# Turning all of batch 1's attention output inside block 0, so that block 1's first product starts in 512 columns

## The chip, the cores and the metric

The kernel runs on one core of a Trainium2 chip. The metric is device time in microseconds of one execution. A profiled execution also gives a span, from its first instruction to its last, and the trace that the profile is read from. Engines are named as the profile names them: PE (matrix products and transposes), PEld (its weight loads), DVE and ACT (the two vector-like engines), POOL and SP (here mostly issuers of transfers).

## What is computed

Two stages follow each other. q, k and v have 8 batches, 8 heads, 576 positions and 64 features.

```python
q_p = concat(relu(q) * cos, relu(q) * sin)           # per position, 64 -> 128 features; k_p alike
kv  = einsum('bhsf,bhsd->bhfd', k_p, v)              # k^T v, one 128 x 64 matrix per head
z   = k_p.sum(axis=positions)
x   = (q_p @ kv) / (q_p @ z + 1e-6)                  # attention output, 576 x 512 per batch
h   = x @ w_in                                       # 512 -> 2048
out = (h * sigmoid(1.702 * h)) @ w_out               # 2048 -> 512
```

All inputs and the output are float32; the kernel computes its products in bf16 with float32 sums.

## The kernel before

The work is cut by batch into eight blocks. Of each batch's 576 positions 512 go through the block in four chunks of 128 (c = 0 to 3); the last 64 (c = 4) are put aside in `xt` and treated together for all batches at the end. The order of every engine's instructions is written out by hand (`manual_schedule`, line 48): an engine runs its instructions in the order of the program, and what it has to wait for is found from the tiles that it reads and writes.

The steps, by function:

- `trig` and `trig_q` make the relu times cos and sin features of k and q, in `kr` and `qn`; `vcopy(i0, i1)` (L157) casts v into `vt`, for head pairs i0 to i1, on DVE or with `act=True` on ACT.
- `qturn_pe(c)` (L167) turns chunk c of q with PE transposes into a PSUM tile, `qevac(c)` (L174) copies it into `qT` (on DVE, or on ACT with `act=True`). For batch 1 the PSUM tiles are the two halves of an `at` tile (`at_homes`, L183).
- `kv_mm` (L202, instructions at L207) is k^T v: 72 products of 64 rows by 65 columns. `kv_evac` (L210, L212) copies the result to `kvs` on DVE.
- `num_mm(c)` (L226, L230) multiplies chunk c of q by `kvs`, 8 products of 65 columns into an `at` tile. `num_div(c)` (L248) divides on DVE in three instructions: `den` (L236), `inv` (L238), `xn` (L254).
- `xturn_mm(c)` (L269, L274) turns `xn` with 4 PE transposes into a free part of the same `at` tile, and `xturn_evac(b, c)` (L276, L280) copies it to `xT` on ACT. `xturn_dma` (L282, L285) does the turning by a transfer from SP instead.
- `mm1(b, fc)` (L303) is one 128-wide slice of x times w_in: 4 products of 512 columns (`mm1_part`, L291, L295), and `gelu` (L300) on ACT into a `g` tile. A block has 16 slices. `mm1_part(b, fc, t0, t1)` can do the same for one chunk, 4 products of 128 columns.
- `mm2(b, t, lo, hi)` (L327, L332) adds slices lo to hi of the second product for chunk t, one 512-column product each. With hi = 16 the sum is complete: ACT copies it to `ysb` (L336) and POOL sends it out (L340).

PSUM has two pools: `pmm` with four buffers (products) and `pat` with two `at` buffers, handed out in turn. The third `at` tile asked for has to wait until the first has been read.

Block 0 is different from the others because batch 1's attention is worked in between its products. The 64 products of `mm2(0, ...)` (L458 to L503) are interleaved with batch 1's q transposes, k^T v, `num_mm` and the first transposes of x. When block 0's products end, two of the four chunks of batch 1's x are turned. `start_block(1, opened=True)` (L355) then begins block 1 chunk by chunk, in 128 columns, for its first four slices, and turns chunks 2 and 3 between these parts; `start_block(0)` does the same for block 0. Blocks 2 to 7 have their x turned by transfers during the block before, and run all 16 slices in 512 columns (L507 on).

Of the kernel before, what the change touches and what calls it, by code (L numbers as in the profile page):

```python
# [19 lines left out]
def kernel(  # L20
# [14 lines left out]
    FC = d_ff // 128  # L35
# [75 lines left out]
    def w_in_of(kc, fc):  # L111
        return w_in_v[fc // 4][:, kc, fc % 4, :]

    def load(t, src, b, eng=nc.gpsimd):
        eng.dma_start(out=t, in_=src_of(src, b))
# [41 lines left out]
    def vcopy(i0, i1, act=False):  # L157
        o = vt[:, :, i0:i1, 0:64].rearrange("p j i e -> p i j e")
        i = vf[:, i0:i1].rearrange("p i (j e) -> p i j e", e=64)
        if act:  # L160
            nc.scalar.activation(o, i, AF.Copy)
        else:
            nc.vector.tensor_copy(o, i)
# [10 lines left out]
    def qevac(c, act=False):  # L174
        n = min(2 * c + 2, NS) - 2 * c
        o = qT[:, :, ds(c * 128, n * 64)].rearrange("f h (j p) -> f j h p", j=n)
        i = tps.pop(c)[:, 0:n].rearrange("f j i (hh p) -> f j (i hh) p", hh=2)
        if act:
            nc.scalar.activation(o, i, AF.Copy)
        else:  # L180
            nc.vector.tensor_copy(o, i)

    def at_homes():  # L183
        t = pat.tile([128, 2, 512], F32, name="at")
        return [t[:, u].bitcast(BF16).rearrange("p (j i f) -> p j i f", j=2, i=NI) for u in range(2)]
# [24 lines left out]
    def kv_evac(i0, i1, n=65):  # L210
        o = st["kvs"][:, :, i0:i1, 0:n]
        nc.vector.tensor_copy(o, st["ps", i0].rearrange("p hh (i e) -> p hh i e", e=65)[:, :, :, 0:n])  # L212
# [13 lines left out]
    def num_mm(c):  # L226
        ps = pat.tile([128, 2, 512], F32, name="at")
        for h in range(H):
            i, hh = divmod(h, 2)
            nc.tensor.matmul(ps[:, h // 4, ds((h % 4) * 65, 65)], qT[:, h, ts(c, 128)],  # L230
                             st["kvs"][:, hh, i, 0:65], start=True, stop=True)
        nums[c] = [ps]
# [15 lines left out]
    def num_div(c, inv=None):  # L248
        ps = nums[c][0]
        pv = ps[:, :, 0:260].rearrange("p a (h e) -> p a h e", h=4)  # L250
        if inv is None:
            inv = inv_of(pv[:, :, :, 64])
        xn = small.tile([128, 2, 4, 64], BF16, name="xn", bufs=4)
        nc.vector.tensor_tensor(xn, pv[:, :, :, 0:64],  # L254
                                inv.unsqueeze(3).to_broadcast([128, 2, 4, 64]), op=MUL)
        nums[c].append(xn)
# [12 lines left out]
    def xturn_mm(c):  # L269
        ps, xn = nums[c]  # L270
        xv = xn.rearrange("p a h e -> p (a h e)")
        for kc in range(KC):
            o = ps[:, kc // 2, ds(264 + (kc % 2) * 64, 64)].bitcast(BF16)
            nc.tensor.transpose(o, xv[:, ts(kc, 128)], ident)  # L274

    def xturn_evac(b, c):  # L276
        ps = nums.pop(c)[0]
        i = ps[:, :, 264:392].bitcast(BF16).rearrange("p a (k t) -> p a k t", k=2)
        o = x_of(b, c).rearrange("p (a k) t -> p a k t", a=2)
        nc.scalar.activation(o, i, AF.Copy)  # L280

    def xturn_dma(b, c):  # L282
        xn = nums.pop(c)[1]
        n = 128 if c < 4 else 64
        nc.sync.dma_start_transpose(out=x_of(b, c), in_=xn[0:n].rearrange("p a h e -> p (a h e)"))  # L285
# [5 lines left out]
    def mm1_part(b, fc, t0, t1):  # L291
        if t0 == 0:
            hp[fc] = pmm.tile([128, MT], F32, name="mm")
        for kc in range(KC):
            nc.tensor.matmul(hp[fc][:, t0:t1], w_in_of(kc, fc), x[b][:, kc, t0:t1],  # L295
                             start=(kc == 0), stop=(kc == KC - 1))

    def gelu(fc):
        g = gpool.tile([128, MT], BF16, name="g")
        nc.scalar.activation(g, hp.pop(fc), AF.Gelu_apprx_sigmoid)  # L300
        gT[fc] = g

    def mm1(b, fc):  # L303
        mm1_part(b, fc, 0, MT)
        gelu(fc)
# [21 lines left out]
    def mm2(b, t, lo, hi, c0=0, c1=d_model):  # L327
        if lo == 0:
            yp[t, c0] = pmm.tile([128, d_model], F32, name="mm")
        for fc in range(lo, hi):  # L330
            w = gT[fc][:, ts(t, 128)] if t < 4 else gl_t[:, fc, ts(t - 4, 128)]
            nc.tensor.matmul(yp[t, c0][:, c0:c1], w, w_out_sb[:, fc, c0:c1],  # L332
                             start=(fc == 0), stop=(fc == FC - 1))
        if hi == FC:
            ysb = ypool.tile([128, d_model], F32, name="ysb")
            nc.scalar.activation(ysb[:, c0:c1], yp[t, c0][:, c0:c1], AF.Identity)  # L336
            for p0, n, dst in rows(b, t):
                last = b == B - 1 and t != 4 and (t, p0) != (5, 0)
                eng = nc.sync if last else nc.gpsimd
                eng.dma_start(out=dst[:, c0:c1], in_=ysb[p0:p0 + n, c0:c1])  # L340
# [11 lines left out]
    def vt_rhs(r, i, j):  # L352
        return vt[r, j, i, 0:65]

    def start_block(b, opened=False):  # L355

        if not opened:
            xturn_mm(0)
            xturn_evac(b, 0)
            num_mm(2)  # L360
            num_div(2)
            xturn_mm(1)
            xturn_evac(b, 1)
        def part(c, *fcs):
            for fc in fcs:
                mm1_part(b, fc, c * 128, c * 128 + 128)

        part(0, 0, 1, 2, 3)
        num_mm(3)
        num_div(3)  # L370
        xturn_mm(2)
        xturn_evac(b, 2)
        part(1, 0, 1, 2, 3)
        xturn_mm(3)
        xturn_evac(b, 3)
        num_mm(4)
        num_div(4)
        xturn_dma(b, 4)
        part(2, 0, 1, 2)
        part(3, 0, 1)  # L380
        part(2, 3)
        part(3, 2, 3)
        for fc in range(4):
            gelu(fc)
        mm1(b, 4)


    w = idle(12)
    for j in (0, 1):
        trig(kr, kf, j)  # L390
# [46 lines left out]
    qevac(4)  # L437
    idle(1)
    x_open(0)
    start_block(0)  # L440


    load(kf, k, 1)
# [15 lines left out]
        mm2(0, t, 0, 4)  # L459
    mm2(0, 0, 4, 8)  # L460
    mm2(0, 1, 4, 8)
    ha = at_homes()
    qturn_pe(0, ha[0])
    qturn_pe(1, ha[1])
    qevac(0)
    qevac(1, act=True)
    mm2(0, 2, 4, 8)
    mm2(0, 3, 4, 8)
    hb = at_homes()
    qturn_pe(2, hb[0])  # L470
    qturn_pe(3, hb[1])
    vcopy(0, 2)
    vcopy(2, 4, act=True)
    qevac(2)
    qevac(3, act=True)
    load_q(2, nc.gpsimd)
    load(kf, k, 2, nc.gpsimd)
    load(vf, v, 2, nc.gpsimd)
    mm2(0, 0, 8, 12)
    mm2(0, 1, 8, 12)  # L480
    hc = at_homes()
    qturn_pe(4, hc[0])
    qevac(4)
    kv_open()
    kv_mm(0, 4, vt_rhs, 0, 65)
    kv_evac(0, 4)
    mm2(0, 2, 8, 12)
    mm2(0, 3, 8, 12)
    num_mm(0)
    num_div(0)  # L490
    num_mm(1)
    num_div(1)
    x_open(1)
    mm2(0, 0, 12, 16)
    mm2(0, 1, 12, 16)
    xturn_mm(0)
    xturn_evac(1, 0)
    mm2(0, 2, 12, 16)
    xturn_mm(1)
    xturn_evac(1, 1)  # L500
    num_mm(2)
    num_div(2)
    mm2(0, 3, 12, 16)  # L503
    start_block(1, opened=True)


    for b in range(1, B):  # L507
        nb = b + 1 if b + 1 < B else None
        f0 = 5 if b == 1 else 0
        for fc in range(f0, FC):  # L510
            if nb is not None and fc == f0:
                for c in range(5):
                    trig_q(c)
                    qturn_dma(c)
                if nb + 1 < B:
                    load_q(nb + 1)
            if nb is not None and fc == f0 + 1:
                for j in range(NS if b > 1 else 5):
                    trig(kr, kf, j)
                vcopy(0, 4 if b > 1 else 2)  # L520
            mm1(b, fc)
            if b == 1 and fc in (7, 9, 11, 13):
                trig(kr, kf, (fc + 3) // 2, act=True)
        if b == 1:
            vcopy(2, 4, act=True)
        if nb is None:
            for fc in range(FC):
                mm1_tails(fc)
            for t in (4, 5, 6, 7):
                mm2(b, t, 0, FC)  # L530
            for t in range(3):
                mm2(b, t, 0, FC)
            mm2(b, 3, 0, FC, 0, 256)
            mm2(b, 3, 0, FC, 256, 512)
            continue
        x_open(nb)
        lag = 1 if b == 1 else 0
        for u in range(8):
            if u == lag:
                kv_open()  # L540
                kv_mm(0, 4, vt_rhs, 0, 65)
                kv_evac(0, 4)
            if 0 <= u - lag - 1 < 5:
                num_mm(u - lag - 1)
                num_div(u - lag - 1)
                xturn_dma(nb, u - lag - 1)
            mm2(b, u // 2, 8 * (u % 2), 8 * (u % 2) + 8)
        if nb + 1 < B:
            load(kf, k, nb + 1, nc.sync)
            load(vf, v, nb + 1, nc.sync)  # L550
# [30 lines left out]
```

## Time and profile before

| | us |
|---|---|
| median of 3 runs (lowest to highest) | 292.51 (292.34 to 292.56) |
| the profiled execution, its time | 292.51 |
| the profiled execution, its span | 290.8 |
| PE busy | 284.3 |
| ACT busy | 132.9 |
| DVE busy | 124.1 |
| POOL busy | 37.8 |

The span is 1.7 us shorter than the time of the same execution; what lies around the span is taken as constant. The profiled execution's time is also the median of the runs. In the timeline a row gives the start, the length from the first start to the last end, the engine, the line, the operation, the tiles as output<-input, and the number of instructions that the row merges. Products on PE overlap: one lasts longer than the distance to the next, so the cost of a group is read from its start to the start of the group after it.

### The profile page before, as it was taken

To read this page: it belongs to the slowest core of one execution; us is meant where nothing else is said; L and a number is where in the kernel's file an instruction comes from. 1 tells how busy PE (TensorE), PEld (TensorE's weight loads), DVE (VectorE), ACT (ScalarE), POOL (GpSimd) and SP (SyncE) were. 2 spreads that over 40 slices of the span, in tenths; PEclk is the share of its full clock that TensorE was granted. 3 is DMA by queue.
4 is the path that set the end of the run, shared out by engine and by line. 5 is a ranking of instruction groups with operands and counts; after the bars stand their busy time and mean duration, and the time that the engine had idled before them with its cause. 6 is when DMAs were issued, how large, how long until landed. Compare 5 with 4: busy or idle time off the path is not lost.

```text
span 290.8 us, 5789 instructions
## 1 busy us (share of the span) xinstructions
PE 284.3 (98%) x2330; PEld 154.8 (53%) x2330; DVE 124.1 (43%) x356; ACT 132.9 (46%) x232; POOL 37.8 (13%) x71
## 2 busy tenths in 40 slices
PE   7989999999999999999999999999999999999995
PEld 2775466755555554555455545554555455544444
DVE  4953645842648363826582567156624200000000
ACT  7957654693156214721463136412651167751111
POOL 6650044101210001001100110011000100002000
PEclk9999999999999999999999999999999999999999
DMA  7999999684689958975699469756975400002322
GB/s 250 244 214 287 372 267 363 172 181 128 126 225 306 220 132 276 260 197 145 225 277 227 122 192 335 184 143 152 379 94 74 117 36 3 0 0 44 87 88 72
DMA packets 67771, 52.48 MB, mean 180 GB/s; under 512 B 47969, under 2 KB 57953, under 8 KB 67745
## 3 DMA queue, kind: packets, MB, share of 16 engines
q1 hardware_dynamic: 60320, 32.52, 45.2%
q0 software_dynamic: 7424, 19.60, 23.6%
q8 instruction: 18, 0.29, 0.4%
q14 instruction: 9, 0.07, 0.1%
HBM read 36.70 MB, written 9.44 MB: 159 GB/s over the span
## 4 chain that ended last, share of the span: by engine, by line
PE 92%; DMA 5%; DVE 1%; POOL 1%; issue 0%; ACT 0%; ACTq 0%
PE mm L332 43%; PE mm L295 38%; PE mm L312 5%; DMA w_in<-in_moe_w_in_dram 3%; PE at L230 3%; PE at L207 3%; DMA kf<-in_k_dram 1%; PE at L171 1%; POOL vb L132 1%; DVE xn L254 0%; PE at L274 0%; DVE inv L238 0%; ACT ysb L336 0%; DVE den L236 0%; POOL gate L130 0%
## 5 line engine op out<-in xcount | busy, mean ns | idle before, releaser
L332 PE MATMUL mm<-w_out_sb,g 128*128 128x512 bf16 (+1 forms) x528 | 117.9, 373 | 0.0
L295 PE MATMUL mm<-xT,w_in 128*128 128x512 bf16 (+1 forms) x608 | 112.9, 345 | 0.2 <-DMA w_in<-in_moe_w_in_dram 0.2
L300 ACT ACTIVATE g<-mm 128x512 bf16<-128x512 f32 x128 | 75.1, 598 | 30.4 <-PE mm L295 30.2
L295 PEld LDWEIGHTS <-w_in 128*128 128x128 bf16 x608 | 61.6, 113 | 49.6 <-DMA w_in<-in_moe_w_in_dram 0.3
L332 PEld LDWEIGHTS <-g 128*128 128x128 bf16 x528 | 48.7, 97 | 49.6
L336 ACT ACTIVATE ysb<-mm 128x512 f32<-128x512 f32 (+1 forms) x37 | 21.7, 586 | 109.7 <-PE mm L332 106.7
L340 POOL DMA_DIRECT2D out_dram<-ysb x39 | 21.2, 547 | 205.6 <-ACT ysb L336 203.6
L142 DVE TENSOR_SCALAR kr<-kf,cosw 128x256 bf16<-128x256 f32 x64 | 22.5, 351 | 30.3 <-DMA kf<-in_k_dram 30.3
L254 DVE TENSOR_TENSOR xn<-at,inv 128x512 bf16<-128x512 f32 x40 | 27.7, 691 | 1.7 <-PE at L230 0.4
L142 DVE TENSOR_SCALAR kr<-kf,sinw 128x256 bf16<-128x256 f32 x64 | 22.6, 354 | 0.0
L236 DVE TENSOR_SCALAR den<-at 128x8 f32<-128x8 f32 x39 | 6.5, 166 | 34.4 <-PE at L230 34.4
L230 PEld LDWEIGHTS <-qT 128*128 128x128 bf16 x320 | 14.6, 97 | 8.1 <-issue 0.8
L212 DVE CAST kvs<-at 128x520 bf16<-128x520 f32 (+1 forms) x9 | 5.7, 635 | 28.9 <-PE at L207 28.9
L230 PE MATMUL at<-kvs,qT 128*128 128x65 bf16 x320 | 15.9, 193 | 0.7 <-ACT xT L280 0.7
L155 DVE TENSOR_SCALAR qn<-qf,sinw 128x512 bf16<-128x512 f32 (+1 forms) x30 | 14.4, 480 | 0.0
L155 DVE TENSOR_SCALAR qn<-qf,cosw 128x512 bf16<-128x512 f32 (+1 forms) x30 | 14.3, 476 | 0.0
L312 PE MATMUL mm<-xt,w_in 128*128 128x512 bf16 x64 | 14.0, 379 | 0.0
L332 PE MATMUL mm<-w_out_sb,gl_t 128*128 128x512 bf16 x64 | 14.0, 379 | 0.0
L313 ACT ACTIVATE gl_t<-mm 128x512 bf16<-128x512 f32 x16 | 9.6, 597 | 4.2 <-PE mm L312 4.2
L312 PEld LDWEIGHTS <-w_in 128*128 128x128 bf16 x64 | 7.2, 113 | 6.6
L207 PEld LDWEIGHTS <-kr 64*128 64x128 bf16 x576 | 9.3, 94 | 2.7 <-issue 2.5
L332 PEld LDWEIGHTS <-gl_t 128*128 128x128 bf16 x64 | 6.3, 98 | 7.5
(63 smaller groups left out, 115.4 us busy)
## 6 DMA issues: line engine op xcount, KB each, us to landing
kf<-in_k_dram SPq DMA_DIRECT2D x5, 1152.0 KB, 6.9
vf<-in_v_dram SPq DMA_DIRECT2D x5, 1152.0 KB, 9.6
qf<-in_q_dram SPq DMA_DIRECT2D x5, 1024.0 KB, 6.2
out_dram<-ysb POOLq DMA_DIRECT2D x20, 256.0 KB, 2.8
out_dram<-ysb POOLq DMA_DIRECT2D x19, 128.0 KB, 4.1
kf<-in_k_dram POOLq DMA_DIRECT2D x2, 1152.0 KB, 11.7
vf<-in_v_dram POOLq DMA_DIRECT2D x2, 1152.0 KB, 16.5
w_in<-in_moe_w_in_dram POOLq DMA_DIRECT2D x4, 512.0 KB, 10.2
```

The lines of the kernel that those rows point to most:

```text
L142: eng.tensor_scalar(o, i, 0.0, w[:, j:j + 1], op0=MAX, op1=MUL)
L155: nc.vector.tensor_scalar(o, i, 0.0, sc, op0=MAX, op1=MUL)
L207: nc.tensor.matmul(st["kv", i][:, hh, ds(col, n)], kr[r, j, i, :], rhs(r, i, j), start=(j == 0), stop=(j == NS - 1))
L230: nc.tensor.matmul(ps[:, h // 4, ds((h % 4) * 65, 65)], qT[:, h, ts(c, 128)], st["kvs"][:, hh, i, 0:65], start=True, stop=True)
L254: nc.vector.tensor_tensor(xn, pv[:, :, :, 0:64], inv.unsqueeze(3).to_broadcast([128, 2, 4, 64]), op=MUL)
L295: nc.tensor.matmul(hp[fc][:, t0:t1], w_in_of(kc, fc), x[b][:, kc, t0:t1], start=(kc == 0), stop=(kc == KC - 1))
L300: nc.scalar.activation(g, hp.pop(fc), AF.Gelu_apprx_sigmoid)
L312: nc.tensor.matmul(hps, w_in_of(kc, fc), xt[:, kc, :], start=(kc == 0), stop=(kc == KC - 1))
L313: nc.scalar.activation(gl_t[:, fc, :], hps, AF.Gelu_apprx_sigmoid)
L332: nc.tensor.matmul(yp[t, c0][:, c0:c1], w, w_out_sb[:, fc, c0:c1], start=(fc == 0), stop=(fc == FC - 1))
L336: nc.scalar.activation(ysb[:, c0:c1], yp[t, c0][:, c0:c1], AF.Identity)
L340: eng.dma_start(out=dst[:, c0:c1], in_=ysb[p0:p0 + n, c0:c1])
```

## The change

`start_block` is gone. Block 0's copy of it stands in line, with `num_mm(4)`/`num_div(4)` ahead of `xturn_mm(3)`/`xturn_evac(0, 3)`. In block 0's second product batch 1's k^T v moves up, directly behind q's turns 0 to 3, and both halves of `vcopy` of batch 1 go to DVE; q's turn 4 goes behind k^T v. `num_mm` of chunks 0 and 1 moves up into the third quarter (slices 8 to 12), and in the last quarter (slices 12 to 16) the `num_mm` of chunks 2, 3 and 4 and the x turns of chunks 1, 2 and 3 stand between the four groups of four products, so that all four chunks of batch 1's x are turned inside block 0. Block 1 then runs all its 16 slices in 512 columns.

```diff
-    def start_block(b, opened=False):
...
-        part(0, 0, 1, 2, 3)
-        num_mm(3)
-        num_div(3)
-        xturn_mm(2)
-        xturn_evac(b, 2)
-        part(1, 0, 1, 2, 3)
-        xturn_mm(3)
-        xturn_evac(b, 3)
-        num_mm(4)
-        num_div(4)
-        xturn_dma(b, 4)
-        part(2, 0, 1, 2)
...
-        mm1(b, 4)
...
-    start_block(0)
+    xturn_mm(0)
...
+    part(0, 0, 1, 2, 3)
+    num_mm(3)
+    num_div(3)
+    xturn_mm(2)
+    xturn_evac(0, 2)
+    part(1, 0, 1, 2, 3)
+    num_mm(4)
+    num_div(4)
+    xturn_mm(3)
+    xturn_evac(0, 3)
+    xturn_dma(0, 4)
+    part(2, 0, 1, 2)
...
+    mm1(0, 4)
...
     mm2(0, 0, 4, 8)
     mm2(0, 1, 4, 8)
+    mm2(0, 2, 4, 8)
     ha = at_homes()
     qturn_pe(0, ha[0])
     qturn_pe(1, ha[1])
     qevac(0)
     qevac(1, act=True)
-    mm2(0, 2, 4, 8)
+    vcopy(0, 2)
+    vcopy(2, 4)
     mm2(0, 3, 4, 8)
     hb = at_homes()
     qturn_pe(2, hb[0])
     qturn_pe(3, hb[1])
-    vcopy(0, 2)
-    vcopy(2, 4, act=True)
-    qevac(2)
+    qevac(2, act=True)
     qevac(3, act=True)
     load_q(2, nc.gpsimd)
     load(kf, k, 2, nc.gpsimd)
     load(vf, v, 2, nc.gpsimd)
+    kv_open()
+    kv_mm(0, 4, vt_rhs, 0, 65)
+    kv_evac(0, 4)
     mm2(0, 0, 8, 12)
-    mm2(0, 1, 8, 12)
     hc = at_homes()
     qturn_pe(4, hc[0])
     qevac(4)
-    kv_open()
-    kv_mm(0, 4, vt_rhs, 0, 65)
-    kv_evac(0, 4)
+    num_mm(0)
+    num_div(0)
+    mm2(0, 1, 8, 12)
+    num_mm(1)
+    num_div(1)
     mm2(0, 2, 8, 12)
     mm2(0, 3, 8, 12)
-    num_mm(0)
-    num_div(0)
-    num_mm(1)
-    num_div(1)
     x_open(1)
-    mm2(0, 0, 12, 16)
-    mm2(0, 1, 12, 16)
     xturn_mm(0)
     xturn_evac(1, 0)
-    mm2(0, 2, 12, 16)
+    mm2(0, 0, 12, 16)
+    num_mm(2)
+    num_div(2)
     xturn_mm(1)
     xturn_evac(1, 1)
-    num_mm(2)
-    num_div(2)
+    mm2(0, 1, 12, 16)
+    num_mm(3)
+    num_div(3)
+    xturn_mm(2)
+    xturn_evac(1, 2)
+    mm2(0, 2, 12, 16)
+    num_mm(4)
+    num_div(4)
+    xturn_mm(3)
+    xturn_evac(1, 3)
+    xturn_dma(1, 4)
     mm2(0, 3, 12, 16)
-    start_block(1, opened=True)
...
-        f0 = 5 if b == 1 else 0
-        for fc in range(f0, FC):
+        for fc in range(FC):
```

More of the change, by code (lines that the diff above doesn't have):

```diff
@@ L353, in vt_rhs @@
         return vt[r, j, i, 0:65]
-    def start_block(b, opened=False):
-        if not opened:
-            xturn_mm(0)
-            xturn_evac(b, 0)
-            num_mm(2)
-            num_div(2)
[L362 to L366, printed above, removed]
-        part(0, 0, 1, 2, 3)
-        num_mm(3)
-        num_div(3)
-        xturn_mm(2)
-        xturn_evac(b, 2)
-        part(1, 0, 1, 2, 3)
-        xturn_mm(3)
-        xturn_evac(b, 3)
-        num_mm(4)
-        num_div(4)
-        xturn_dma(b, 4)
-        part(2, 0, 1, 2)
[L380 to L384, printed above, removed]
-        mm1(b, 4)
     w = idle(12)
@@ L439, with part @@
     x_open(0)
-    start_block(0)
+    xturn_mm(0)
+    xturn_evac(0, 0)
+    num_mm(2)
+    num_div(2)
+    xturn_mm(1)
+    xturn_evac(0, 1)
+    def part(c, *fcs):
+        for fc in fcs:
+            mm1_part(0, fc, c * 128, c * 128 + 128)
+    part(0, 0, 1, 2, 3)
[10 more added lines that the diff above has]
+    part(2, 0, 1, 2)
+    part(3, 0, 1)
+    part(2, 3)
+    part(3, 2, 3)
+    for fc in range(4):
+        gelu(fc)
+    mm1(0, 4)
     load(kf, k, 1)
@@ L483 @@
     qevac(4)
-    kv_open()
-    kv_mm(0, 4, vt_rhs, 0, 65)
-    kv_evac(0, 4)
+    num_mm(0)
[3 more added lines that the diff above has]
+    num_div(1)
     mm2(0, 2, 8, 12)
     mm2(0, 3, 8, 12)
-    num_mm(0)
-    num_div(0)
-    num_mm(1)
-    num_div(1)
     x_open(1)
-    mm2(0, 0, 12, 16)
-    mm2(0, 1, 12, 16)
     xturn_mm(0)
     xturn_evac(1, 0)
-    mm2(0, 2, 12, 16)
+    mm2(0, 0, 12, 16)
+    num_mm(2)
+    num_div(2)
     xturn_mm(1)
     xturn_evac(1, 1)
-    num_mm(2)
-    num_div(2)
+    mm2(0, 1, 12, 16)
[9 more added lines that the diff above has]
+    xturn_dma(1, 4)
     mm2(0, 3, 12, 16)
-    start_block(1, opened=True)
     for b in range(1, B):
         nb = b + 1 if b + 1 < B else None
-        f0 = 5 if b == 1 else 0
-        for fc in range(f0, FC):
-            if nb is not None and fc == f0:
+        for fc in range(FC):
+            if nb is not None and fc == 0:
                 for c in range(5):
@@ L516 @@
                     load_q(nb + 1)
-            if nb is not None and fc == f0 + 1:
+            if nb is not None and fc == 1:
                 for j in range(NS if b > 1 else 5):
```

## The prediction

> **What bounds the kernel now.** The page first: the span, and the shares of the engines in the chain of work that ended last.
>
> ```profile
> span 290.8 us, 5789 instructions
> PE 92%; DMA 5%; DVE 1%; POOL 1%; issue 0%; ACT 0%; ACTq 0%
> ```
>
> PE carries 92% of the chain, so a change can only save PE work, or time in which PE waits for another engine. The timeline of PE over the stretch that the change touches shows both: block 0's second product starts at 31.38, block 1's at 65.11, and 33.73 us lie between.
>
> ```profile
> 31.38 5.34 PE L332 MATMUL mm<-w_out_sb,g 128*128 128x512 bf16 x24
> 36.56 1.06 PE L171 MATMUL at<-ident,qn 128*128 128x128 bf16 x16
> 39.18 1.06 PE L171 MATMUL at<-ident,qn 128*128 128x128 bf16 x16
> 41.80 0.39 PE L171 MATMUL at<-ident,qn 128*128 128x128 bf16 x4
> 42.20 1.26 PE L207 MATMUL at<-vt,kr 64*128 64x65 bf16 x72
> 43.40 1.90 PE L332 MATMUL mm<-w_out_sb,g 128*128 128x512 bf16 x8
> ...
> 48.43 0.39 PE L274 MATMUL at<-ident,xn 128*128 128x128 bf16 x4
> 48.68 0.40 PE L230 MATMUL at<-kvs,qT 128*128 128x65 bf16 x8
> ...
> 49.78 1.24 PE L295 MATMUL mm<-xT,w_in 128*128 128x128 bf16 x16
> 50.85 0.41 PE L230 MATMUL at<-kvs,qT 128*128 128x65 bf16 x8
> 51.10 0.38 PE L274 MATMUL at<-ident,xn 128*128 128x128 bf16 x4
> 51.32 1.06 PE L295 MATMUL mm<-xT,w_in 128*128 128x128 bf16 x16
> 52.48 0.40 PE L274 MATMUL at<-ident,xn 128*128 128x128 bf16 x4
> 52.72 0.41 PE L230 MATMUL at<-kvs,qT 128*128 128x65 bf16 x8
> 52.96 12.31 PE L295 MATMUL mm<-xT,w_in 128*128 128x128 bf16 x80
> 65.11 1.89 PE L332 MATMUL mm<-w_out_sb,g 128*128 128x512 bf16 x8
> ```
>
> From start to start: a 512-column product takes (36.56 - 31.38)/24 = 0.216. The merged row at 52.96 holds 32 products of 128 columns and 48 of 512, 12.15 in all; less 48 x 0.2158 = 10.36 that leaves 1.79, or 0.056 for one of 128 columns. Eight `num_mm` products take 0.24 (52.72 to 52.96), four transposes 0.22 (51.10 to 51.32), sixteen 0.89 (39.18 - 8 x 0.216 - 36.56), k^T v 1.20 (42.20 to 43.40).
>
> What is longer than that is waiting. After the four transposes at 41.80 k^T v could start at 42.02 and starts at 42.20: 0.18. The sixteen short products at 49.78 need 0.90 and take 1.07: 0.17. Those at 51.32 need 0.90 and the next start is 1.16 later: 0.26. The rows of the other engines that end these waits:
>
> ```profile
> 38.38 1.02 ACT L179 ACTIVATE qT<-at 128x1024 bf16<-128x1024 bf16 x1 [0.97 <-DVE qT L181]
> 39.30 1.16 ACT L161 ACTIVATE vt<-vf 128x1152 bf16<-128x1152 f32 x1
> 41.13 1.02 ACT L179 ACTIVATE qT<-at 128x1024 bf16<-128x1024 bf16 x1 [0.67 <-DVE qT L181]
> 49.98 0.60 ACT L336 ACTIVATE ysb<-mm 128x512 f32<-128x512 f32 x1 [0.26 <-PE mm L332]
> 37.66 0.69 DVE L181 COPY qT<-at 128x1024 bf16<-128x1024 bf16 x1 [0.82 <-PE at L171]
> 38.26 0.91 DVE L163 CAST vt<-vf 128x1152 bf16<-128x1152 f32 x1
> 43.50 0.70 DVE L212 CAST kvs<-at 128x520 bf16<-128x520 f32 x1 [0.85 <-PE at L207]
> 51.73 0.69 DVE L254 TENSOR_TENSOR xn<-at,inv 128x512 bf16<-128x512 f32 x1
> ```
>
> The ACT `qT` copy ends at 42.15 (k^T v needs its PSUM buffer), the `ysb` copy at 50.58 (a `pmm` buffer), `xn` of chunk 3 at 52.42 (the turn of chunk 3). PE goes on some 0.05 after each. With 0.03 in front of `num_mm(2)` (48.43 + 0.22, start 48.68) and 0.06 scattered over hand-offs the waits are 0.70.
>
> **The change, part by part.** *512 columns in block 1.* 64 products of 128 columns, 64 x 0.056 = 3.58, become 16 of 512, 16 x 0.2158 = 3.45. The gain is 0.13. PE's work in the stretch is then 128 x 0.2158 = 27.62 for the long products, 2.88 for 52 transposes, 1.20 for k^T v and 5 x 0.24 for `num_mm`: 32.90, against 33.03 before.
>
> *k^T v behind q's turns.* I count from the start of the second product, kept at 31.38 for the moment. 28 products end at 37.42, the turns 0 and 1 at 38.31, four products at 39.18, the turns 2 and 3 at 40.07. k^T v then takes the `at` buffer that held turns 0 and 1. Before, `qevac(0)` began 1.10 after the start of its turns (36.56 to 37.66) and `qevac(1)` on ACT followed it. So: turns at 37.42, DVE 38.52 to 39.21, ACT 39.24 to 40.26, PE at 40.31. New wait 0.24, where 0.18 was.
> The copies of v come next on DVE: `vcopy(0, 2)` from 39.12, and, at the 0.91 of the row above (less some 0.08 of overlap, as 37.66 + 0.69 and 38.26 show), `vcopy(2, 4)` from 39.95 to 40.86. The second half of k^T v starts at 40.31 + 0.60 = 40.91, just behind it. Half of `vcopy` was on ACT for 1.16; had it stayed there it would now hold up `qevac(2)`. Bounds of this part: 0 if PE loses nothing, 0.9 if k^T v had to wait for a whole further copy. I take 0.24, since each link has its own row.
> `load(vf, v, 2)` on POOL waits for the second copy, as it did for ACT's (ended 40.46): 0.4 later. Its cover is below.
>
> *q's turn 4 and `num_mm(0)`, `num_mm(1)`.* k^T v ends at 41.51. `kvs` is copied in 0.70, by 42.3, beside four long products and the turn 4 (to 42.6). `qevac(2)` and `qevac(3)`, both on ACT now, run from 40.28 (1.10 after their turns' start, again) to 42.2, at 1.02 each; turn 4 needs their buffer at 42.4. No wait. `num_mm(0)` at 42.6 follows; `num_mm(1)` at 43.7 needs `qevac(4)`, one half of a copy of 0.69 that starts at about 42.8: over by then.
>
> *The last quarter.* Four products, `num_mm(c+2)` and the turn of chunk c+1 take 0.86 + 0.24 + 0.22 = 1.32 a round. Two loops must fit. One through ACT: a turn needs 0.43 until `xT` starts and 0.60 to copy (first fence below), so `num_mm(2)` may start 1.08 after the start of turn 0; PE has the turn and four products, 1.08, in between. An exact tie, three times and once more for block 1's first product. One through DVE: `num_mm(3)` started at 50.85 and the turn that waited for its `xn` at 52.48, so a turn may start 1.63 after its `num_mm`, with 0.24 + 0.22 + 0.86 + 0.24 = 1.56 of PE work between. A wait of 0.06 in the first such round and some 0.05 in the rest. Sum of the new waits: 0.24 + 0.11 = 0.35.
>
> ```profile
> 17.59 1.06 PE L295 MATMUL mm<-xT,w_in 128*128 128x128 bf16 x16
> 18.75 0.40 PE L274 MATMUL at<-ident,xn 128*128 128x128 bf16 x4
> 19.23 12.32 PE L295 MATMUL mm<-xT,w_in 128*128 128x128 bf16 x80
> 17.36 0.38 PE L274 MATMUL at<-ident,xn 128*128 128x128 bf16 x4
> 17.79 0.60 ACT L280 ACTIVATE xT<-at 128x512 bf16<-128x512 bf16 x1 [1.12 <-PE at L274]
> 19.19 0.60 ACT L280 ACTIVATE xT<-at 128x512 bf16<-128x512 bf16 x1 [0.80 <-PE at L274]
> ```
>
> The stretch becomes 32.90 + 0.35 = 33.25 against 33.73: 0.48 less.
>
> *Block 0's start.* `num_mm(4)` moves into the wait for `xn` between 18.49 and 18.75, so the parts of chunks 2 and 3 begin at 18.97, not 19.23. But chunk 3 (12 products, 0.67, later) needs the ACT copy of 19.19 to 19.79, which is not moved: it begins at 19.84 instead of 19.90. Gain 0.06 of 0.26.
>
> *What is moved beside PE.* POOL and SP issue the same transfers in the same order. DVE's work for batch 2 (`trig_q`) starts at about 51.2, three microseconds earlier, and could meet loads not yet landed.
>
> ```profile
> 37.71 0.91 POOL L118 DMA_DIRECT2D qf<-in_q_dram  x1 [16.27 <-ACT qn L140]
> DMA to landing us min/median/max: 7.9/7.9/7.9
> 39.43 0.76 POOL L115 DMA_DIRECT2D kf<-in_k_dram  x1
> DMA to landing us min/median/max: 10.8/10.8/10.8
> 40.75 0.75 POOL L115 DMA_DIRECT2D vf<-in_v_dram  x1 [0.55 <-ACT vt L161]
> DMA to landing us min/median/max: 12.2/12.2/12.2
> 54.21 0.48 DVE L155 TENSOR_SCALAR qn<-qf,cosw 128x512 bf16<-128x512 f32 x1
> ```
>
> q lands at 45.6 (needed at 51.2), k at 50.2 (needed at 55), v at 53 or 53.4 (needed at 58); the results are due only at batch 2's k^T v, 67 before. That cover gone, PE would wait for k^T v by what a load is late. I cost it at nothing.
>
> **Sum.** 0.48 + 0.06 = 0.54 less. The profiled execution took 292.51, which is also the median of the runs: 292.51 - 0.54 = 291.97, say 291.95. That is 0.19% faster, while 0.2% (0.585 us) is about what a measurement of this kernel can tell from no change: the forecast lies on that line.
>
> **Rivals.**
> *The ties fall on PE's side.* ACT and DVE are ahead where I count 0.35 of new waits and 0.06 scattered hand-offs: 0.95 less, 291.55. For it: the sums are ties to 0.06. Against: the wait in front of k^T v, 0.24 of it, follows from four measured rows.
> *The waits move.* Each of seven hand-offs (the second half of k^T v, two turns, three `num_mm`, block 1's first product) is late by another 0.06, the size of one hand-off: 0.4 comes back, 292.4. It speaks for it that nothing has slack.
> *The ACT loop doesn't close* (slower). Between the turns ACT now has `xT(c)`, `ysb`, `xT(c+1)` in strict order, 1.2 us of full durations in rounds of 1.32. If an `xT` has to wait behind half a `ysb` (0.30) at all four ties, 4 x 0.30 = 1.2 is lost: 293.15. It decides for slower by over 0.2% from 0.28 a tie on (0.54 + 0.585 over four). Against: the `ysb` row at 49.98 began 0.2 after its last product, and at that pace ACT is free within 0.05 of each turn's end.
> *Short products are set by their weight loads.* The load of `w_in` lasts 113 ns in this row:
>
> ```profile
> L295 PEld LDWEIGHTS <-w_in 128*128 128x128 bf16 x608 | 61.6, 113 | 49.6 <-DMA w_in<-in_moe_w_in_dram 0.3
> ```
>
> If each 128-column product cost its load, 64 x 0.113 = 7.2 would become 3.45, with 3.8 less: 288.6. The 12.15 of the merged row leave 0.056, half a load, so loads overlap; I give it 2 in 100.
> The Trainium skill, page "TensorE: Matmul & The Clock Gate", section "Back-to-back issue gap", has a rule of this kind: in a real stream of loads and products about 81 ns for 128 columns and 131 ns for 512. By it the step would save 64 x 81 - 16 x 131 ns, an estimate of 3.1 us instead of 0.13. The trace disagrees at both ends, with 56 and 216 ns.
>
> **How the numbers follow.** Forecast 0.68, a little over half of it beyond the line (0.38 faster, 0.30 the same); ties on PE's side 0.13 (faster); weight loads 0.02 (faster); the waits move 0.09 (the same); the ACT loop 0.08 (slower). Faster 0.53, same 0.39, slower 0.08. The range goes from 291.5, just past the first rival, to 292.55, just past the second; it leaves out the slower case and the weight loads.
>
> **What would show it.** Right: `num_mm` rows between four-product rows up to about 50; no 128-column rows of L295 after 21; block 1's second product at about 64.6; k^T v at about 40.3 with the ACT `qT` copy ending just before. Wrong: gaps of over 0.1 in front of the L274 or L230 rows between 45 and 51, an L163 copy well over 0.91, a `qn` row of DVE released by a transfer, or a k^T v of batch 2 that waits.

## The result, and the profile after

The changed kernel takes 291.81 us (median of 17 runs, 291.59 to 292.75), the kernel before 292.33 beside it. The ratio is 0.9983, 95% interval 0.9976 to 0.9991, and the medians differ by 0.52 us. That is just under the 0.2% (0.585 us) that the prediction named as what a measurement can tell, but the whole interval lies below 1: the kernel is a little faster.

The first profile of the changed kernel fell on an execution of 292.75, the slowest of the 17. The page:

```profile
span 291.0 us, 5656 instructions
PE 91%; DMA 3%; ACT 2%; DVE 1%; issue 1%; SPq 1%; ACTq 0%
```

The span is longer than before (291.0 against 290.8), and the reason lies ahead of everything that was changed. The DVE row that starts on the second part of batch 0's q was not held up before; in this profile it waited for its transfer, and batch 0 ran 0.7 to 1.2 us later from there on. First the row of the kernel before, then that of this profile:

```profile
9.43 0.35 DVE L142 TENSOR_SCALAR qn<-qf,cosw 128x256 bf16<-128x256 f32 x1
```

```profile
10.67 0.35 DVE L142 TENSOR_SCALAR qn<-qf,cosw 128x256 bf16<-128x256 f32 x1 [0.84 <-DMA qf<-in_q_dram]
...
32.05 6.21 PE L332 MATMUL mm<-w_out_sb,g 128*128 128x512 bf16 x27
...
65.33 1.03 PE L332 MATMUL mm<-w_out_sb,g 128*128 128x512 bf16 x3
```

The stretch from block 0's second product to block 1's, read inside the same profile, is free of that: 65.33 - 32.05 = 33.28, against 33.73 before. (Some records are missing, so that the counts 27 and 3 fall short of 28 and 8; starts are what is read.) The chain is PE's at 91%, as it was.

A second profile of the same kernel opened without the delay and has all its records. Its PE timeline:

```profile
31.19 6.21 PE L332 MATMUL mm<-w_out_sb,g 128*128 128x512 bf16 x28
...
38.99 1.06 PE L171 MATMUL at<-ident,qn 128*128 128x128 bf16 x16
40.13 1.26 PE L207 MATMUL at<-vt,kr 64*128 64x65 bf16 x72
41.33 1.04 PE L332 MATMUL mm<-w_out_sb,g 128*128 128x512 bf16 x4
42.20 0.39 PE L171 MATMUL at<-ident,qn 128*128 128x128 bf16 x4
42.42 0.41 PE L230 MATMUL at<-kvs,qT 128*128 128x65 bf16 x8
...
45.72 1.03 PE L332 MATMUL mm<-w_out_sb,g 128*128 128x512 bf16 x4
46.58 0.41 PE L230 MATMUL at<-kvs,qT 128*128 128x65 bf16 x8
46.83 0.39 PE L274 MATMUL at<-ident,xn 128*128 128x128 bf16 x4
47.05 1.03 PE L332 MATMUL mm<-w_out_sb,g 128*128 128x512 bf16 x4
47.92 0.40 PE L230 MATMUL at<-kvs,qT 128*128 128x65 bf16 x8
48.21 0.40 PE L274 MATMUL at<-ident,xn 128*128 128x128 bf16 x4
48.45 1.03 PE L332 MATMUL mm<-w_out_sb,g 128*128 128x512 bf16 x4
49.31 0.41 PE L230 MATMUL at<-kvs,qT 128*128 128x65 bf16 x8
...
50.65 13.97 PE L295 MATMUL mm<-xT,w_in 128*128 128x512 bf16 x64
64.46 1.89 PE L332 MATMUL mm<-w_out_sb,g 128*128 128x512 bf16 x8
```

ACT's rows of the same profile, the copies of q's turns 1, 2 and 3 and then the four copies of x's turns:

```profile
39.05 3.03 ACT L179 ACTIVATE qT<-at 128x1024 bf16<-128x1024 bf16 x3 [1.46 <-DVE qT L181]
...
45.92 0.60 ACT L280 ACTIVATE xT<-at 128x512 bf16<-128x512 bf16 x1 [3.83 <-PE at L274]
...
47.27 0.59 ACT L280 ACTIVATE xT<-at 128x512 bf16<-128x512 bf16 x1
...
48.65 0.60 ACT L280 ACTIVATE xT<-at 128x512 bf16<-128x512 bf16 x1
...
50.00 0.59 ACT L280 ACTIVATE xT<-at 128x512 bf16<-128x512 bf16 x1
```

What to see: the stretch is 33.27. Turns 2 and 3 start at 38.99 and take 0.89, so k^T v could start at 39.88 and starts at 40.13: one wait of 0.25. It ends where the prediction put it, 0.05 to 0.06 after ACT's copy of turn 1 (39.05 + 1.02 = 40.07). In the last quarter each group begins where the one before it ends, but for 0.05 at 48.21 (47.92 + 0.24 = 48.16), and each `xT` copy ends 0.06 before the product that needs it: 46.52 before 46.58, 47.86 before 47.92, 49.25 before 49.31, 50.59 before 50.65. Block 1's sixteen slices are one row, 13.81 from start to start.

### The profile page after: what moved, and what is told of

It reads as the page before. It is cut to its first block, busy times and chain, and to the rows that moved or that the text cites. A ratio compares the mean times of both kernels' runs of the same rounds, so it can differ in the third digit from the quotient of the medians.

```text
span 291.0 us, 5656 instructions
## 1 busy us (share of the span) xinstructions
PE 281.8 (97%) x2247; PEld 153.0 (53%) x2282; DVE 123.7 (43%) x356; ACT 133.1 (46%) x232; POOL 37.8 (13%) x71
## 4 chain that ended last, share of the span: by engine, by line
PE 91%; DMA 3%; ACT 2%; DVE 1%; issue 1%; SPq 1%; ACTq 0%
PE mm L332 42%; PE mm L295 37%; PE mm L312 5%; PE at L230 3%; PE at L207 3%; DMA qf<-in_q_dram 3%; ACT g L300 1%; PE at L274 1%; DVE qn L142 1%; DVE qT L181 0%; PE at L171 0%; ACT qT L179 0%; SPq L62 0%; DVE xn L254 0%; ACT xT L280 0%
## 5 line engine op out<-in xcount | busy, mean ns | idle before, releaser
L332 PE MATMUL mm<-w_out_sb,g 128*128 128x512 bf16 (+1 forms) x506 | 116.7, 372 | 1.3 <-issue 0.2
L295 PEld LDWEIGHTS <-w_in 128*128 128x128 bf16 x560 | 59.8, 113 | 50.9
L312 PEld LDWEIGHTS <-w_in 128*128 128x128 bf16 x64 | 7.2, 113 | 6.6
```

Of the source, the lines that this page charges most:

```text
L312: nc.tensor.matmul(hps, w_in_of(kc, fc), xt[:, kc, :], start=(kc == 0), stop=(kc == KC - 1))
```

## The experiments

The theory is the prediction's: PE's rows plus a handful of waits, each ended by a named copy on ACT or DVE, give the time to about a tenth of a microsecond. The rivals: the gain is block 0's start, or the columns; the waits are elsewhere; products are set by their weight loads; the place of a copy or ACT's order has slack. "Stretch" is the time from the start of block 0's second product to that of block 1's. The kernel before was measured again beside each of them on the same chip. The row "xT behind ysb" has only two executions, the others 10 to 12.

| kernel | median | before | ratio (95%) | stretch |
|---|---|---|---|---|
| start alone | 292.48 | 292.37 | 1.0001 (0.9989 to 1.0013) | 33.73 |
| second product alone | 291.98 | 292.37 | 0.9979 (0.9967 to 0.9992) | 33.44 |
| changed kernel, second profile | 292.04 | 292.35 | 0.9983 (0.9970 to 0.9996) | 33.27 |
| turns earlier | 291.53 | 292.37 | 0.9974 (0.9959 to 0.9990) | 33.11 |
| short columns | 292.44 | 292.37 | 0.9993 (0.9980 to 1.0007) | 33.75 |
| copy on ACT | 292.64 | 292.35 | 1.0013 (1.0004 to 1.0023) | 34.08 |
| xT behind ysb | 296.94 | 292.35 | 1.0158 (1.0139 to 1.0176) | 38.51 |
| POOL after the copies | 291.78 | 292.37 | 0.9980 (0.9971 to 0.9989) | 33.27 |
| turns earlier, POOL after | 291.65 | 292.37 | 0.9982 (0.9967 to 0.9997) | 33.11 |

**The changed kernel once more.**

> The changed kernel once more, for a second profile: the first had its opening transfers land late, so that batch 0's first product began later than before. If that is chance and not the change, this profile's span is about 290.1, its first x turn starts at 14.3 to 14.6, and the stretch from the second product's start to block 1's is again 33.25 to 33.3 us. If the change causes it, the start is late again, at 15.4, and the time 292.7.

Its first turn of x starts at 14.57 and its span is 290.1, with the stretch at 33.27. The same kernel opens on time here, so the change does not force the late opening. Two later kernels open late in their profiles too (first turn of x at 15.33 in "turns earlier", 15.17 in "short columns"); whether the change makes this more frequent is not shown. The stretch is free of it and is the measure to use. The medians of this second set of runs differ by only 0.31 us, with the same ratio, 0.9983: medians alone don't fix the gain to a tenth of a microsecond.

**Block 0's start alone**, and the rest alone.

```diff
-        xturn_mm(3)
-        xturn_evac(b, 3)
-        num_mm(4)
-        num_div(4)
+        if not opened:
+            num_mm(4)
+            num_div(4)
+        xturn_mm(3)
+        xturn_evac(b, 3)
+        if opened:
+            num_mm(4)
+            num_div(4)
```

> The kernel before, with one part of the change: in block 0's start num_mm(4) and num_div(4) stand ahead of the turn of chunk 3. If the prediction's count holds, the parts of chunk 2 begin 0.26 us earlier, chunk 3 still waits for ACT's xT copy, and 0.06 to 0.10 us are gained: 292.25, not to be told from before by the time, but by a wait of about 0.2 in the merged row of the parts. Rival: the whole 0.26 is kept (292.07) and the start is half of the gain.

The time can't tell 0.1 us, as said. The profile can, when read from `num_mm(3)`, which comes ahead of the swap, to the second product's start. The row of `num_mm(3)` before, and then the rows of this kernel, last the `xT` copy of ACT that chunk 3 waits for:

```profile
17.12 0.41 PE L230 MATMUL at<-kvs,qT 128*128 128x65 bf16 x8
```

```profile
16.99 0.41 PE L230 MATMUL at<-kvs,qT 128*128 128x65 bf16 x8
...
18.85 12.49 PE L295 MATMUL mm<-xT,w_in 128*128 128x128 bf16 x79
31.17 5.34 PE L332 MATMUL mm<-w_out_sb,g 128*128 128x512 bf16 x23
19.05 0.60 ACT L280 ACTIVATE xT<-at 128x512 bf16<-128x512 bf16 x1 [0.76 <-PE at L274]
```

31.38 - 17.12 = 14.26 before, 31.17 - 16.99 = 14.18 here: 0.08. The parts of chunk 2 begin 0.25 earlier, counted in the same way (2.11 after `num_mm(3)` before, 1.86 here), and the merged row, 12.15 long from start to start before, takes 12.32: 0.17 of waiting came into it. ACT's copy for chunk 3 stays where it was, 2.06 after `num_mm(3)` (19.05 - 16.99; before 19.19 - 17.12 = 2.07). By the profile the rival that all of the 0.26 is kept is out.

The second product alone (the changed kernel with `xturn_mm(3)` and `xturn_evac(0, 3)` again ahead of `num_mm(4)`):

> The changed kernel with block 0's start as before: only the new order of the second product and block 1 in 512 columns. Count: the stretch from the second product's start to block 1's takes 33.25 to 33.3 us, as in the changed kernel, and 0.45 to 0.48 are gained against 33.73: 291.87. Rival, that the start carries the gain: 292.1 to 292.3.

The median, 291.98, lies between the count and the rival's range, and its interval doesn't separate the two. The profiles do: block 0's start alone gained 0.08, while the stretch, which holds nothing of that start, is shorter than before by 0.29 here and by 0.46 in the changed kernel. So most of the gain is the second product's and block 1's. The expected stretch was missed: 33.44, not 33.25 to 33.3. The excess is inside k^T v:

```profile
38.82 1.06 PE L171 MATMUL at<-ident,qn 128*128 128x128 bf16 x16
39.96 1.44 PE L207 MATMUL at<-vt,kr 64*128 64x65 bf16 x72
41.33 1.04 PE L332 MATMUL mm<-w_out_sb,g 128*128 128x512 bf16 x3
38.77 1.86 DVE L163 CAST vt<-vf 128x1152 bf16<-128x1152 f32 x2
```

k^T v takes 1.37 where 1.20 is its cost. The two copies of v end at 40.63. The second half of k^T v follows the first after 0.54 where nothing holds it (in the second profile of the changed kernel), so it was due at 40.50; it starts at 40.68, 0.05 after the copies. In the second profile of the changed kernel the same pair took 1.58. The last experiments go into that.

**The wait ahead of k^T v.**

```diff
     mm2(0, 1, 4, 8)
-    mm2(0, 2, 4, 8)
     ha = at_homes()
...
     vcopy(2, 4)
-    mm2(0, 3, 4, 8)
+    mm2(0, 2, 4, 8)
     hb = at_homes()
...
     qevac(3, act=True)
+    mm2(0, 3, 4, 8)
     load_q(2, nc.gpsimd)
```

> The changed kernel with q's turns 0 and 1 and their copies put four products earlier (ahead of mm2(0, 2, 4, 8)), and mm2(0, 3, 4, 8) put behind the turns 2 and 3, just ahead of k^T v. If the wait of 0.25 in front of k^T v is that for the ACT copy that frees its PSUM buffer, it is gone and nothing takes its place: 0.25 less than the changed kernel, 291.55, the stretch 33.03. Rival: the second copy of v, or the copies of turns 2 and 3, are late next, and the wait comes back in the middle of k^T v or in front of turn 4: 291.8.

The lowest median of all, 291.53. The stretch is 33.11: 0.16 less than the changed kernel, not 0.25, so that the median came out on the expected 291.55 is in part luck. Nothing else is late. k^T v now follows long products, and that hand-off costs 0.10, as the kernel before shows in block 1, where k^T v comes behind eight products of `mm2`:

```profile
66.94 1.26 PE L207 MATMUL at<-vt,kr 64*128 64x65 bf16 x72
```

65.11 + 1.73 = 66.84, and the row starts at 66.94. It is the same in every later block of that profile: 0.31 from the start of the last long product, of which 0.216 is the product. `num_mm`, which has products of as many columns but 128 rows, starts behind long products without it (45.72 + 0.86 = 46.58); what makes the difference is not shown. The kernel with this edit and POOL held back (below) has the rows in full:

```profile
38.02 1.06 PE L171 MATMUL at<-ident,qn 128*128 128x128 bf16 x16
38.92 1.03 PE L332 MATMUL mm<-w_out_sb,g 128*128 128x512 bf16 x4
39.88 1.26 PE L207 MATMUL at<-vt,kr 64*128 64x65 bf16 x72
```

38.92 + 0.86 = 39.78, and k^T v starts at 39.88.

**The columns.** In block 1, for every slice:

```diff
-            mm1(b, fc)
+            if b == 1:
+                for c in range(4):
+                    mm1_part(b, fc, c * 128, c * 128 + 128)
+                gelu(fc)
+            else:
+                mm1(b, fc)
```

> The changed kernel with all 16 slices of block 1 in products of 128 columns (256 instead of 64), each slice's four parts one after the other, so that the disputed cost is four times the one that the change removed. At 0.056 us each they take 14.34 instead of 13.81: 0.53 more than the changed kernel, 292.3. Rival, products set by their weight loads of 0.113: 28.9, 15 more, 307. By the Trainium skill, page TensorE: Matmul & The Clock Gate, section Back-to-back issue gap, an estimate from 81 and 131 ns would be 12.4 us more.

```profile
51.25 14.46 PE L295 MATMUL mm<-xT,w_in 128*128 128x128 bf16 x256
65.54 1.89 PE L332 MATMUL mm<-w_out_sb,g 128*128 128x512 bf16 x7
```

256 short products take 65.54 - 51.25 = 14.29, or 0.0558 each, 0.48 more than 64 long ones. For the 64 short products that the change removed that is 0.12. The rival by weight loads (15 us more) is out. So is, for this kernel, the pair of figures in the Trainium skill's page "TensorE: Matmul & The Clock Gate", section "Back-to-back issue gap", 81 and 131 ns in a real stream; the stream here keeps 56 and 216 ns.

**The place of the second copy of v.**

```diff
-    vcopy(2, 4)
+    vcopy(2, 4, act=True)
```

> The changed kernel with the second copy of v back on ACT, behind the copy of turn 1. Count: the copy ends at ACT's 1.02 + 1.16 instead of DVE's 1.70 after the copy of turn 0, so the second half of k^T v waits about 0.46; the copies of turns 2 and 3 move back by 0.9 to 1.0 and hold up turn 4 by another 0.36: 0.82 more than the changed kernel, 292.6. Rival, that the place of the copy is covered: 291.8.

PE's rows, then ACT's:

```profile
40.22 0.72 PE L207 MATMUL at<-vt,kr 64*128 64x65 bf16 x36
41.27 0.72 PE L207 MATMUL at<-vt,kr 64*128 64x65 bf16 x36 [0.33 <-ACT vt L161]
41.93 1.04 PE L332 MATMUL mm<-w_out_sb,g 128*128 128x512 bf16 x4
43.10 0.38 PE L171 MATMUL at<-ident,qn 128*128 128x128 bf16 x4
40.07 1.16 ACT L161 ACTIVATE vt<-vf 128x1152 bf16<-128x1152 f32 x1
41.12 1.93 ACT L179 ACTIVATE qT<-at 128x1024 bf16<-128x1024 bf16 x2
```

Both predicted waits are there: the second half of k^T v starts 1.05 after the first, not 0.54 (0.51), and turn 4 waits for the copies of turns 2 and 3 to end at 43.05 (41.93 + 0.86 = 42.79; 0.31). Together they are 0.82, and the stretch is 34.08, 0.81 longer than the changed kernel's. With the copy left on ACT, as before, the new order would have been a little slower than the kernel before (34.08 against 33.73 in the stretch).

**ACT's order in the last quarter**, the mechanism of the slower rival, forced.

```diff
-    xturn_evac(1, 0)
     mm2(0, 0, 12, 16)
+    xturn_evac(1, 0)
     num_mm(2)
```

and so in each of the four rounds.

> The changed kernel with each xT copy of batch 1 issued on ACT behind the ysb copy of the same round instead of ahead of it. Count: from the end of four products 0.20 to the ysb copy, 0.49 to the xT copy, 0.60 for it, 0.05 to PE: each of the three num_mm and block 1's first product waits 1.34 instead of 0 to 0.02: 5.3 us more, 297.1. Rival, that ACT's order has slack of a ysb copy: under 1 us more.

```profile
45.58 1.03 PE L332 MATMUL mm<-w_out_sb,g 128*128 128x512 bf16 x4
47.77 0.40 PE L230 MATMUL at<-kvs,qT 128*128 128x65 bf16 x8 [1.17 <-ACT xT L280]
50.43 0.40 PE L230 MATMUL at<-kvs,qT 128*128 128x65 bf16 x8 [1.17 <-ACT xT L280]
53.09 0.40 PE L230 MATMUL at<-kvs,qT 128*128 128x65 bf16 x8 [1.17 <-ACT xT L280]
55.75 13.97 PE L295 MATMUL mm<-xT,w_in 128*128 128x512 bf16 x64 [1.17 <-ACT xT L280]
```

Four waits: 47.77 - 45.58 - 0.86 = 1.33 from start to start (the profile's 1.17 counts from the end of the products). The stretch is 5.24 longer than the changed kernel's, and the median of the two executions 4.6 us above the kernel before. The rival of slack is out: the loop through ACT has none, and the order chosen, xT ahead of ysb, is what makes it tie.

**POOL beside the copies of v.**

```diff
+    nc.gpsimd.tensor_copy(gate[0:1, 2:3], vt[0:1, 8, 3, 0:1])
     load_q(2, nc.gpsimd)
```

> The changed kernel with POOL's issues of batch 2's loads held until both copies of v on DVE are done (POOL first copies one element of vt, so it waits for them). Theory: the copies took 1.58 to 1.86 for the two because POOL issued beside them, and take 0.75 + 0.68 = 1.43 alone; k^T v still starts when the ACT copy of turn 1 ends, so the time stays that of the changed kernel, 291.8 to 292.0, and the second half of k^T v can't be late. The loads land some 2.5 us later, still ahead of DVE's use. Rival: the spread of the copies has nothing to do with POOL, and the two take 1.58 or more again.

The pair and POOL's second issue, first of the changed kernel (second profile), then of this one:

```profile
38.94 1.58 DVE L163 CAST vt<-vf 128x1152 bf16<-128x1152 f32 x2
38.79 1.17 POOL L120 DMA_DIRECT2D qf<-in_q_dram  x1
```

```profile
38.97 1.42 DVE L163 CAST vt<-vf 128x1152 bf16<-128x1152 f32 x2
41.90 0.72 POOL L120 DMA_DIRECT2D qf<-in_q_dram  x1
```

1.42, two lone copies of 0.75 that overlap a little, and POOL's issue is 0.72 in place of 1.17. The rival is out: what spreads the copies comes with POOL's issues. Whether it is the issues themselves or the transfers that they start is not separated here. The time and the stretch (33.27) are those of the changed kernel, and the loads, issued over 2 us later, held up no row of DVE.

Both edits together:

> The turns 0 and 1 four products earlier, as in the experiment before, together with POOL's issues held until the copies of v are done. Both theories: the stretch from the second product's start to block 1's is 33.1 us (0.17 less than the changed kernel), the two copies take 1.43, and the time is 291.6, 0.2 less than the changed kernel and 0.7 less than before. Rival: the later loads hold DVE up, and the gain is lost: 291.9 or more.

Stretch 33.11 and copies of 1.42 as expected; the median is 291.65, 0.72 below the kernel before. That its ratio (0.9982) is no better than the changed kernel's comes from one execution of 293.81 among eleven. Whether this one or the kernel without the POOL edit is the faster can't be told from these runs; by the stretch both beat the changed kernel by 0.16.

## Why the prediction was right

- *The bound.* PE's rows and a few waits: the stretch was put at 33.25 and took 33.27 and 33.28. The time, 291.95, came out as 291.81 and, in the second set of runs, 292.04. That the stretch hits to 0.02 is in part luck: of the 0.35 of new waits 0.30 are there (0.25 and 0.05), and some 0.07 over other hand-offs, which the sum left out, stands in for the rest.
- *512 columns*: 0.13 predicted, 0.12 by the count of 256 short products.
- *k^T v behind q's turns*: a wait of 0.24 predicted, 0.25 found; the experiment that takes it away shows that only 0.16 of it can be had there, because the hand-off from long products costs 0.10. The prediction had no such term. In the changed kernel k^T v follows transposes and starts 0.05 after ACT's copy; whether a hand-off cost lies inside that wait can't be seen.
- *The second copy of v*: this is the weakest term. The pair was priced at one value, 1.74 (0.91 for each copy with 0.08 of overlap), and k^T v's second half was put 0.60 after its first, which left 0.05 to spare. In the profiles with POOL's issues beside it the pair took 1.58 to 1.86, and the second half follows after 0.54, so there is nothing to spare: it lost 0.02 or nothing in the two profiles of the changed kernel and 0.17 in that of the second product alone. That the changed kernel showed no more is luck. The direction (it must leave ACT) was right: on ACT it costs 0.81.
- *The last quarter*: the DVE loop's wait of 0.06 is the 0.05 at 48.21, and the 0.05 put down for its other rounds isn't there; the four ties of the ACT loop hold to 0.01. The slower rival needed 0.28 a tie; forced, the ties cost 1.33 each, so the mechanism is real, but ACT takes the copies in the order that avoids it.
- *Block 0's start*: 0.06 predicted of 0.26 that moved, 0.07 to 0.08 found, for the reason given: the ACT copy of chunk 3 doesn't move.
- *The covers*: DVE's first `qn` row for batch 2, here in the second profile, names no transfer that it waited for:

```profile
50.80 0.48 DVE L155 TENSOR_SCALAR qn<-qf,cosw 128x512 bf16<-128x512 f32 x1
```

  Even 2 us later, with POOL held back, the loads were in time.
- *The rivals*: short products set by their weight loads are out by the count of 256 short products. (The time given for that rival, 288.6, should be 288.3: 292.51 less 0.41 for the other terms and 3.8.) The ties came out on neither side: neither 0.41 more was gained nor 0.4 lost.
- *The chances* gave 0.53 to a gain beyond 0.2%. It came out just short of that line, at 0.52 of 0.585 us, on the side that had 0.39. With the forecast on the line itself, which side it would be was nearly an even bet.

## What to carry to other kernels

Where one engine is the bound, add its rows from start to start, then list for every wait the copy that ends it; here a reordering could be priced from the rows of the kernel before to one or two tenths of a microsecond, and a stretch inside the profile measures it better than the whole time, in which the opening transfers alone moved by up to a microsecond. Narrow products were nearly as good as wide ones here; their removal was worth 0.12 of the 0.46 us in the stretch, and the rest came from waits, above all those of turning x piece by piece. When work is moved forward, look at which engine's queue its copies stand in: the same copy on ACT instead of DVE, or behind its neighbour instead of ahead, would have turned the gain into a loss.

## What the runs showed of the hardware

The copy of v (128 x 1152, float32 to bf16, on DVE) lasts 0.75 when POOL issues nothing beside it, as both copies did in the two kernels with POOL held back; alongside POOL's transfers it lasted 0.91 in the kernel before and 1.07 with block 0's start alone. POOL's issue of the small q transfer lasts 0.72 when no copy of v runs beside it, and 1.17 in the second profile of the changed kernel, where a copy of v starts 0.15 after it and keeps its 0.75. The kernel with the copy on ACT shows the same: its one DVE copy took 0.75 and POOL's issue 1.18. In the second product alone the copy starts 0.31 after the issue, and there the issue keeps its 0.72 and the copy takes 1.00. The Trainium skill's page "SBUF — State Buffer", section "Who interferes with whom", says that DVE's faster copies and POOL share one pair of ports and that whoever comes first holds it for its whole instruction. The rows agree that the two hold each other up: with POOL's issues moved away, the pair went from 1.58 to 1.42 and POOL's 1.17 to 0.72. They don't bear out the rest as it stands: POOL's issue begins first in all three of these cases and is the one held up in two of them, and the delays (0.16 to 0.45) are parts of an instruction, not its whole length. An issue that needs the ports only part of the way through would fit, but no run here tells which part that is.
